# Two small VectorE operations moved to other engines, and three steps moved in the order, in an induced-attention and ELU-FFN kernel

## The chip, the core and the metric

The kernel runs on one core of a Trainium2 chip. Its time is device microseconds (us) of one execution. The core has five engines that each run their own queue in order: TensorE (PE in the profile; its weight loads have a row of their own, PEld), VectorE (DVE), ScalarE (ACT), GpSimd (POOL) and SyncE (SP, which here issues all DMAs). An instruction starts when its engine has come to it and the semaphores that it waits on have arrived; whatever stands behind it in that engine's queue waits too.

## What is computed

```python
# x: 4 x 12480 x 128, inducing: 32 x 128, w_in: 128 x 2048, w_out: 2048 x 128
def mab(q, kv):                                  # attention, 1/sqrt(128) as scale
    s = scale * (q @ kv.T);  s -= s.max(-1)
    a = exp(s);  a /= a.sum(-1) + 1e-9
    return a @ kv
h   = mab(inducing, x)     # first attention:  32 rows look at 12480 tokens -> h: 32 x 128
y   = mab(x, h)            # second attention: every token looks at those 32 rows
g   = elu(y @ w_in)        # 2048 wide
out = g @ w_out            # 49920 x 128, float32
```

x and inducing come as float32, the two weight matrices as float64, which the kernel itself converts to float32 at its start.

## The kernel before, in words

**Tiling.** Each of the four batches is cut into 25 blocks of 512 or 480 tokens, and the blocks are put in 7 groups of 2 to 4 blocks for the attention. The FFN of a block goes in 8 pairs of 128-wide slices of its 2048 columns. A pair is the unit in which the whole program is written: there are 4 x 25 x 8 = 800, numbered n = 0 to 799. The tokens reach the FFN as second-softmax weights (tile `stk`, three stacked parts), and the projected h times w_in is the matrix `hw`, so that `y @ w_in` is one product.

**One pair.** `ffn_in` (L609) is two matmuls into a two-bank PSUM tile `ph`, of which there are three, and an exponential on ScalarE (L617). `ffn_mid` (L623) takes max and min on VectorE. With that the PSUM tile is free again, unless the pair is of kind D. `ffn_split` (L632) makes the high part `gh` on ScalarE. `ffn_low` makes the low part `gl`: on VectorE (L639, kind D) or on GpSimd (L644 and L649, kind P); kind N has no split, and only L644. The kinds of the 8 pairs are `PDNPDPND`. `ffn_out` (L671) is six matmuls (four for N) into the block's PSUM bank `po`, five pairs later; after a block's last pair VectorE transposes the bank (L679) and SyncE sends it out.

**Order.** In iteration n the program issues `ffn_in(n)`, `ffn_mid(n-1)`, `ffn_split(n-1)`, `ffn_low(n-2)`, then goes on with steps that are under way, then `ffn_out(n-5)`, then starts the side steps whose place n/8 has come. A side step is a generator: `yield k` lets it rest for k pairs. The places of side steps are blocks counted from the batch's first, and stand in `attend` and `first_half`. On PE, VectorE and ScalarE the instructions stay in the order in which the program issues them; on GpSimd and SyncE a scheduler at build time may move them.

**Side steps.** For batch b they compute the first attention of batch b+1 and the second attention of groups to come. First attention: `scores` (L310 to L327, running maxima in `pm`), `bias_of` (the maximum over the four copies of a row, brought together by a product `apart` and a matmul with `nsel4`; once after group 2, once after group 6), `weights_of` (exponential, sums in `es`), `e_of` (a transpose), `gather` (L399, 32 small matmuls, then L409, L411 or L416 adds the bank to `h`), `sum_es`, `share_of` (one matmul, then r = 1/(sum + 1e-9) on VectorE, L439 and L440), `norm_h` (L446), `spread_h` (L452, L455), `project_h`, `stack_h`. Second attention, per group: `attend_scores` (L527, L537), `attend_exp`, `attend_norm` (row sum L558, + 1e-9 L559, reciprocal L560, product on GpSimd L561), `attend_stack` (transpose L570, parts L580 and L582, DMAs into `stk`).

**PSUM.** All eight banks are used: three `ph` of two banks, and two `po` banks, which the blocks take in turn. After the opening a side step's matmul goes into the `po` bank that the next block will take (`bank`). So the next block's first `ffn_out` must wait until VectorE has read the side step's result, and a side step must wait until the one before it in the same bank has been read. `po` of block k begins with pair 8k+5.

**Opening.** The first attention of batch 0 and the conversion of the weights are not hidden behind anything. Their steps are written out in the string `FIRST`: x and y are the two transpose halves of a group's tokens, s and m its scores and maxima, w its weights, e its transpose, g and h its gather and the addition; b0 to b2 the biases; A to E the conversion of a piece of a weight matrix (A takes it apart on VectorE and ScalarE, B makes the scale on GpSimd, C puts bits together on VectorE, D multiplies on VectorE and GpSimd, E splits w_out on ScalarE and GpSimd); l0 to l3 the second attention of block 0 alone, a0 to a3 that of the rest of group 0; u0 and on are the pairs, among which the rest of the steps stand. When the string is used up, after some 12 pairs, the list `steady` is filled, and side steps take the other form where a line asks for it.

Of the kernel before, what the change touches and what calls it, by code (L numbers as in the profile page):

```python
# [9 lines left out]
F32 = mybir.dt.float32  # L10
# [3 lines left out]
AF = mybir.ActivationFunctionType  # L14
# [3 lines left out]
P = 128  # L18
# [14 lines left out]


FIRST = """
    A0 A1 B0 x0 y0 C0 B1 x1 s0 D0 y1 C1 m0 s1 D1 x2 m1 y2 x3 s2 m2 y3 b0 w0 s3 x4 w1 m3 e0
    y4 w2 e1 x5 s4 m4 A2 g0 y5 e2 h0 g1 b1 x6 y6 w3 g2 s5 w4 h1 h2 e3 B2 s6 e4 m5 room A3 g3
    m6 b2 B3 g4 h3 w5 w6 C2 e5 D2 sum g5 e6 h4 g6 C3 h5 share h6 D3 norm spread l0 project
    l1 A4 stack l2 A5 l3 B4 a0 u0 a1 C4 B5 u1 a2 D4 C5 u2 E4 a3 D5 A6 u3 B6 E5 u4 C6 u5 D6
    A7 u6 B7 E6 u7 C7 u8 D7 u9 E7 u10 u11 u12  # L40
"""


# [1 line left out]
def kernel(  # L45
# [8 lines left out]
    nc = tc.nc  # L54
# [28 lines left out]
    EPS = 1e-9  # L83
# [9 lines left out]
    const = ctx.enter_context(tc.tile_pool(name="const", bufs=1))  # L93
# [19 lines left out]
    steady = []  # L113

    def bank(name, take=False):
        if not steady and not take:
            return ps_h.tile([P, 2, 512], F32, tag="ph", name=name)[:, 0]
        t = ps_o.tile([P, 512], F32, tag=f"po{turn[0] % 2}", name=name)
        if take:
            turn[0] += 1  # L120
        return t
# [22 lines left out]
    ps = bank("ps_ind")  # L144
# [9 lines left out]
    WS = 512  # L154
    rebias = const.tile([P, 1], F32, name="rebias")
    nc.gpsimd.memset(rebias, -896.0)
    largest = const.tile([P, 1], F32, name="largest")
    nc.gpsimd.memset(largest, 254.0)

# [134 lines left out]
    def start(b):  # L294
        st = dict(
            pm=small.tile([P, NG], F32, tag="pm", name=f"pm_{b}"),
            es=small.tile([P, NG], F32, tag="es", name=f"es_{b}"),
        )
        nc.gpsimd.memset(st["pm"], -3.0e38)
        nc.gpsimd.memset(st["es"], 0.0)  # L300
        state[b] = st
# [31 lines left out]
    def phases(b):  # L333
        ends = [0, 3, NG - 2, NG] if b == 0 else [0, 3, NG]
        return [range(i, j) for i, j in zip(ends, ends[1:])]
# [4 lines left out]
    def bias_of(b, i):  # L340
        st = state[b]
        n = phases(b)[i].stop
        ps = bank(f"ps_pm_{b}_{i}")
        apart = small.tile([P, 4, NG], F32, tag="apart", name=f"apart_{b}_{i}")
        nc.vector.tensor_tensor(
            out=apart[:, :, :n],
            in0=st["pm"][:, :n].unsqueeze(1).broadcast_to([P, 4, n]),
            in1=mine.unsqueeze(2).broadcast_to([P, 4, n]),
            op=ALU.mult,
        )  # L350
        nc.tensor.matmul(ps[:, : 4 * n], nsel4, apart[:, :, :n], start=True, stop=True)
        yield 1
        bias = small.tile([P, 1], F32, tag=f"bias{i}", name=f"bias_{b}_{i}")
        nc.vector.tensor_reduce(out=bias, in_=ps[:, : 4 * n], axis=AX.X, op=ALU.min)
        st["bias", i] = bias
        if i:
            st["scale", i] = small.tile([P, 1], F32, tag=f"scale{i}", name=f"scale_{b}_{i}")
            nc.scalar.activation(
                st["scale", i], st["bias", i - 1], AF.Exp, bias=bias, scale=-1.0
            )  # L360
# [25 lines left out]
    def e_of(b, g):  # L386
        st = state[b]
        np_, T = GROUPS[g][1] * Q, GROUPS[g][2]
        e = ep.tile([P, T], F32, tag="e", name=f"e_{b}_{g}")
        nc.vector.transpose(e[:np_], st["s", g])  # L390
        st["e", g] = e
# [41 lines left out]
    def share_of(b):  # L433
        st = state[b]
        ps = bank(f"ps_es_{b}")
        nc.tensor.matmul(ps[:, :1], sel4, st["es1"], start=True, stop=True)
        yield 1
        r = small.tile([P, 1], F32, tag="r", name=f"r_{b}")
        nc.vector.tensor_scalar_add(r, ps[:, :1], EPS)  # L439
        nc.vector.reciprocal(r, r)  # L440
        st["r"] = r

    def norm_h(b):
        st = state[b]
        hn = once.tile([P, C], F32, tag="hn", name=f"hn_{b}")
        nc.vector.tensor_scalar_mul(hn, st["h"], st["r"])  # L446
        st["hn"] = hn
# [105 lines left out]
    def attend_norm(b, g):  # L553
        s = state[b]["s2", g]
        np_, U = s.shape[:2]
        eng = nc.gpsimd if steady else nc.vector
        sm = small.tile([P, U], F32, tag="sm2", name=f"sm2_{b}_{g}")[:np_]
        nc.vector.tensor_reduce(out=sm, in_=s, axis=AX.X, op=ALU.add)  # L558
        nc.vector.tensor_scalar_add(sm, sm, EPS)  # L559
        nc.vector.reciprocal(sm, sm)  # L560
        eng.tensor_tensor(  # L561
            out=s, in0=s, in1=sm.unsqueeze(2).broadcast_to([np_, U, Q]), op=ALU.mult
        )
        yield 3
# [133 lines left out]
    def first_half(b):  # L698
        steps = [(0.0, lambda: start(b))]
        at = 0.0  # L700
        for g in range(NG):
            for h in [h for h in range(NH) if HALVES[h][2] == g]:

                room = attend(b - 1, HALVES[h - 1][2])[0][0] - (b - 1) * NBLK + 0.3 if h else 0.0
                at = max(at + 0.5, room)
                steps.append((at, lambda h=h: load_xT(b, h)))
            steps.append((at + 1.1, lambda g=g: scores(b, g)))
            if g + 1 == phases(b)[0].stop:
                first = at + 1.1
        second = at + 1.1  # L710
        end = NBLK - 3.97
        for i, (at, till) in enumerate([(first, second), (second, end)]):
            steps.append((at + 0.2, lambda i=i: bias_of(b, i)))
            at += 0.4
            gap = (till - at) / len(phases(b)[i])
            for g in phases(b)[i]:
                steps.append((at, lambda g=g: weights_of(b, g)))
                steps.append((at + 0.15, lambda g=g: e_of(b, g)))
                steps.append((at + 1.19, lambda g=g: gather(b, g)))
                for j, v in enumerate(range(0, GROUPS[g][2] // Q, UP)):  # L720
                    steps.append((at - 0.7 + 0.1 * j, lambda g=g, v=v: load_xm(b, g, v)))
                at += gap
        steps.append((end + 0.3, lambda: room_for_h(b), f"h{b}"))
        steps.append((end + 0.3, lambda: sum_es(b), f"h{b}"))
        steps.append((end + 0.4, lambda: share_of(b), f"h{b}"))
        steps.append((end + 0.6, lambda: norm_h(b), f"h{b}"))
        steps.append((end + 0.8, lambda: spread_h(b), f"h{b}"))
        steps.append((end + 1.1, lambda: project_h(b), f"h{b}"))
        steps.append((end + 1.4, lambda: stack_h(b), f"h{b}"))
        return [((b - 1) * NBLK + v[0], *v[1:]) for v in steps]  # L730
# [150 lines left out]
```

## Time and profile before

| | |
|---|---|
| time, median of 3 runs | 1749.53 us (1749.2 to 1749.7) |
| the profiled execution's own time | 1750.1 us |
| its span, first to last instruction | 1748.3 us |
| mean granted TensorE clock | 0.985 |
| start of pair 0 | 61.2 us |
| time of one batch in the middle (from one stall to the same one in the next batch) | 420.1 us |

A row of a timeline gives start, duration, engine, line, operation, output and inputs, the shapes, the count of merged instructions, and in brackets the time for which the engine had been idle and what it waited for. A row of a group view gives count, busy time and mean duration in ns of one, then the idle time ahead of the group and what ended it. A row of the waits gives total time, times, and the longest one. In the chain of waits "issue" is time in which nothing that the profile shows was waited for. Line numbers are those of the kernel before; in the changed kernel lines are two to nine higher.

### The profile page before, as it was taken

How to read it: one execution, taken by the hardware profiler on the slowest of the kernel's cores; microseconds unless marked ns; L12 is line 12 of the kernel's file. 1: busy time of each engine (PE TensorE's matmuls, PEld its weight loads, DVE VectorE, ACT ScalarE, POOL GpSimd, SP SyncE). 2: the span in 40 equal slices, each digit the busy share in tenths (PEclk: the TensorE clock that was granted, in tenths of full speed). 3: DMA queues.
4: the chain of work that ended last, by engine and by line, in shares of the span. 5: the costliest groups of instructions: out<-in, count | busy, mean ns of one | idle time of the engine just before them, and what ended most of it. 6: DMA issues, size and time to landing. Idle time of an engine off the chain costs nothing.

```text
span 1748.3 us, 22270 instructions
## 1 busy us (share of the span) xinstructions
PE 1652.5 (95%) x7448; PEld 1175.6 (67%) x7448; DVE 1569.1 (90%) x1608; ACT 1384.8 (79%) x1593; POOL 1341.5 (77%) x941
## 2 busy tenths in 40 slices
PE   6589999999999999999999999999999999999998
PEld 4256766767675676667776666666767767676776
DVE  6789999989899999998989999989888999999996
ACT  4468888878787888878787888878878878888886
POOL 4567777877787777877778777877778878887886
PEclk9689999999999999999999999999999999999999
DMA  7254233322225243232323432320312111111111
GB/s 243 47 84 70 59 61 55 61 52 65 66 47 79 36 79 66 41 61 61 79 49 53 62 60 49 77 54 13 79 42 44 36 19 35 28 36 18 35 22 22
DMA packets 384754, 98.10 MB, mean 56 GB/s; under 512 B 364864, under 2 KB 370784, under 8 KB 384384
## 3 DMA queue, kind: packets, MB, share of 16 engines
q1 hardware_dynamic: 384640, 96.68, 28.2%
q8 instruction: 59, 0.97, 0.2%
q14 instruction: 55, 0.45, 0.1%
HBM read 48.94 MB, written 25.56 MB: 43 GB/s over the span
## 4 chain that ended last, share of the span: by engine, by line
PE 74%; DVE 17%; ACT 5%; issue 2%; DMA 1%; POOL 1%; SPq 0%; DVEq 0%; ACTq 0%; POOLq 0%
PE po L671 51%; PE ph L609 18%; DVE e L623 4%; DVE ph L623 3%; ACT e L617 3%; DVE sm L559 2%; DVE gl L639 2%; PE ps_t L527 1%; PE ps_hh L399 1%; ACT gh L632 1%; PE ps_s L310 1%; DVE xT L257 1%; DVE sm L558 1%; PE ps_x L278 1%; DVE pm L327 1%
## 5 line engine op out<-in xcount | busy, mean ns | idle before, releaser
L617 ACT ACTIVATE e<-ph 128x1024 f32<-128x1024 f32 (+1 forms) x800 | 805.0, 1007 | 258.2 <-PE ph L609 249.5
L644 POOL TENSOR_SCALAR e<-e 128x1024 f32<-128x1024 f32 (+1 forms) x500 | 511.0, 1029 | 331.4 <-ACT gh L632 323.5
L649 POOL TENSOR_TENSOR gl<-e,gh 128x1024 fp32r<-128x1024 f32 (+1 forms) x300 | 703.3, 2344 | 16.3
L623 DVE SCALAR_TENSOR_TENSOR e<-ph,e 128x1024 f32<-128x1024 f32 (+1 forms) x500 | 593.3, 1187 | 77.7 <-ACT e L617 76.0
L609 PE MATMUL ph<-stk,hw 128*128 128x512 f32 (+1 forms) x1600 | 561.7, 433 | 45.1 <-DVE e L623 38.2
L671 PE MATMUL po<-gh,wo_h 128*128 128x512 f32 (+1 forms) x1200 | 466.8, 389 | 19.3 <-ACT wo_h L236 9.1
L671 PE MATMUL po<-gh,wo_l 128*128 128x512 f32 (+1 forms) x1200 | 465.8, 388 | 4.2 <-POOL wo_l L237 4.2
L609 PEld LDWEIGHTS ph<-stk,hw 128*128 128x128 f32 x1600 | 291.9, 190 | 226.7 <-DVE e L623 88.6
L623 DVE SCALAR_TENSOR_TENSOR ph<-ph,e 128x1024 f32<-128x1024 f32 (+1 forms) x300 | 358.9, 1196 | 62.7 <-ACT e L617 62.6
L671 PE MATMUL po<-gl,wo_h 128*128 128x512 f32 (+1 forms) x1200 | 368.1, 388 | 0.0
L671 PE MATMUL po<-e,wo_n 128*128 128x512 f32 (+1 forms) x800 | 368.0, 582 | 0.0
L639 DVE SCALAR_TENSOR_TENSOR gl<-ph,gh 128x1024 fp32r<-128x1024 f32 (+1 forms) x300 | 356.0, 1187 | 1.0 <-ACT gh L632 1.0
L632 ACT ACTIVATE gh<-e 128x1024 fp32r<-128x1024 f32 (+1 forms) x300 | 312.1, 1040 | 24.4 <-DVE e L623 24.4
L632 ACT ACTIVATE gh<-ph 128x1024 fp32r<-128x1024 f32 (+1 forms) x300 | 301.1, 1004 | 31.9 <-DVE ph L623 31.6
L671 PEld LDWEIGHTS po<-gh,wo_h 128*128 128x128 f32 x1200 | 226.5, 189 | 67.9 <-ACT wo_h L236 9.5
L671 PEld LDWEIGHTS po<-gh,wo_l 128*128 128x128 f32 x1200 | 226.7, 189 | 49.1 <-POOL wo_l L237 4.9
L671 PEld LDWEIGHTS po<-gl,wo_h 128*128 128x128 f32 x1200 | 226.6, 189 | 43.4 <-POOL gl L649 0.7
L671 PEld LDWEIGHTS po<-e,wo_n 128*128 128x128 f32 x800 | 151.5, 189 | 106.7 <-issue 92.0
L679 DVE STREAM_TRANSPOSE o<-po 128x512 f32<-128x512 f32 (+1 forms) x100 | 68.9, 689 | 4.0 <-PE po L671 4.0
L559 DVE TENSOR_SCALAR sm<-sm 128x16 f32<-128x16 f32 (+3 forms) x28 | 44.9, 1605 | 1.0
L257 DVE STREAM_TRANSPOSE xT<-xq 128x1024 f32<-128x1024 f32 (+2 forms) x39 | 45.4, 1165 | 0.0
L399 PE MATMUL ps_hh<-xm,e 128*32 128x128 f32 (+2 forms) x872 | 32.3, 285 | 2.7 <-DVE e L390 1.6
(96 smaller groups left out, 572.4 us busy)
## 6 DMA issues: line engine op xcount, KB each, us to landing
xm<-in_x_dram SPq DMA_DIRECT2D x32, 512.0 KB, 4.6
out_dram<-o SPq DMA_DIRECT2D x240, 64.0 KB, 2.0
xq<-in_x_dram SPq DMA_DIRECT2D x84, 128.0 KB, 3.7
out_dram<-o SPq DMA_DIRECT2D x160, 60.0 KB, 2.0
stk<-ahi SPq DMA_DIRECT2D x118, 64.0 KB, 2.0
xq<-in_x_dram SPq DMA_DIRECT2D x60, 120.0 KB, 3.4
stk<-ahi SPq DMA_DIRECT2D x80, 60.0 KB, 2.0
stk<-alo SPq DMA_DIRECT2D x59, 64.0 KB, 2.0
```

The source lines that it names most:

```text
L257: nc.vector.transpose(t, xq.rearrange("p u d -> p (u d)"))
L399: nc.tensor.matmul(ps[c * Q : (c + 1) * Q, :C], st["e", g][:np_, u * Q : (u + 1) * Q], st["xm", g, u - u % UP][:np_, u % UP, :], start=(u ...
L559: nc.vector.tensor_scalar_add(sm, sm, EPS)
L609: nc.tensor.matmul(ph[:, i], state[b]["hw"][:, f * P : (f + 1) * P], stacks[b, k], start=True, stop=True,)
L617: nc.scalar.activation(e, ph, AF.Exp, bias=-1.0)
L623: nc.vector.scalar_tensor_tensor(out=v["g"], in0=v["ph"], scalar=1.0, in1=v["e"], op0=ALU.max, op1=ALU.min)
L632: nc.scalar.activation(v["gh"], v["g"], AF.Copy, bias=-1.0)
L639: nc.vector.scalar_tensor_tensor(out=v["gl"], in0=v["g"], scalar=-1.0, in1=v["gh"].bitcast(F32), op0=ALU.add, op1=ALU.subtract,)
L644: nc.gpsimd.tensor_scalar(out=v["e"], in0=v["e"], scalar1=-1.0, scalar2=1.0, op0=ALU.add, op1=ALU.mult)
L649: nc.gpsimd.tensor_sub(v["gl"], v["e"], v["gh"].bitcast(F32))
L671: nc.tensor.matmul(po[:, :T], w, g, start=(cp == 0 and i == 0), stop=(cp == NCP - 1 and i == len(parts) - 1),)
L679: nc.vector.transpose(o.rearrange("p u d -> p (u d)"), po[:, :T])
```

## The change

1. `attend_norm`, after the opening: the addition of 1e-9 is an activation (Identity with a tile `eps` as bias) on ScalarE, one pair after the row sum, and the reciprocal comes one pair after that. In the opening it stays on VectorE. It holds for 27 of 29 calls.
2. `bias_of`, after the opening: the product `apart` runs on GpSimd, and the matmul with what follows it comes three pairs later. It holds for 6 of 9 calls.
3. `first_half`: the first `weights_of` of a phase stands 1.0 block after the phase's start rather than 0.4. The groups of a phase are spread evenly over the rest of it, so all of `weights_of`, `e_of`, `gather` and `load_xm` move by some pairs. `share_of` goes from 0.4 to 0.62 and `norm_h` from 0.6 to 0.75 blocks after the end mark; `spread_h` stays at 0.8.
4. `FIRST` is another order of the same steps.

```diff
@@ FIRST
-    A0 A1 B0 x0 y0 C0 B1 x1 s0 D0 y1 C1 m0 s1 D1 x2 m1 y2 x3 s2 m2 y3 b0 w0 s3 x4 w1 m3 e0
-    y4 w2 e1 x5 s4 m4 A2 g0 y5 e2 h0 g1 b1 x6 y6 w3 g2 s5 w4 h1 h2 e3 B2 s6 e4 m5 room A3 g3
-    m6 b2 B3 g4 h3 w5 w6 C2 e5 D2 sum g5 e6 h4 g6 C3 h5 share h6 D3 norm spread l0 project
-    l1 A4 stack l2 A5 l3 B4 a0 u0 a1 C4 B5 u1 a2 D4 C5 u2 E4 a3 D5 A6 u3 B6 E5 u4 C6 u5 D6
-    A7 u6 B7 E6 u7 C7 u8 D7 u9 E7 u10 u11 u12
+    x0 A0 A1 B0 x1 y0 C0 B1 D0 y1 s0 C1 m0 s1 x2 m1 y2 x3 s2 m2 y3 b0 w0 s3 x4 w1 m3 e0 y4
+    w2 e1 x5 s4 D1 m4 A2 g0 y5 B2 g1 b1 h0 e2 x6 y6 g2 s5 C2 A3 w4 w3 s6 h1 h2 e3 e4 m5 room
+    g3 m6 b2 B3 h3 w5 g4 w6 e5 D2 sum g5 e6 h4 g6 C3 h5 D3 share h6 norm spread l0 A4
+    project l1 A5 l2 l3 B4 B5 a0 stack u0 a1 u1 C4 D4 a2 C5 E4 u2 D5 a3 u3 A6 B6 E5 u4 C6 u5
+    D6 A7 u6 B7 E6 u7 u8 C7 D7 u9 u10 E7 u11 u12
@@ tile_induced_attention__then__elu_ffn_kernel
+    eps = const.tile([P, 1], F32, name="eps")
+    nc.gpsimd.memset(eps, EPS)
@@ bias_of
-        ps = bank(f"ps_pm_{b}_{i}")
         apart = small.tile([P, 4, NG], F32, tag="apart", name=f"apart_{b}_{i}")
-        nc.vector.tensor_tensor(
+        (nc.gpsimd if steady else nc.vector).tensor_tensor(
             out=apart[:, :, :n],
             in0=st["pm"][:, :n].unsqueeze(1).broadcast_to([P, 4, n]),
             in1=mine.unsqueeze(2).broadcast_to([P, 4, n]),
             op=ALU.mult,
         )
+        if steady:
+            yield 3
+        ps = bank(f"ps_pm_{b}_{i}")
         nc.tensor.matmul(ps[:, : 4 * n], nsel4, apart[:, :, :n], start=True, stop=True)
@@ attend_norm
         nc.vector.tensor_reduce(out=sm, in_=s, axis=AX.X, op=ALU.add)
-        nc.vector.tensor_scalar_add(sm, sm, EPS)
+        if steady:
+            yield 1
+            nc.scalar.activation(sm, sm, AF.Identity, bias=eps[:np_])
+            yield 1
+        else:
+            nc.vector.tensor_scalar_add(sm, sm, EPS)
         nc.vector.reciprocal(sm, sm)
@@ first_half
             steps.append((at + 0.2, lambda i=i: bias_of(b, i)))
-            at += 0.4
+            at += 1.0
...
-        steps.append((end + 0.4, lambda: share_of(b), f"h{b}"))
-        steps.append((end + 0.6, lambda: norm_h(b), f"h{b}"))
+        steps.append((end + 0.62, lambda: share_of(b), f"h{b}"))
+        steps.append((end + 0.75, lambda: norm_h(b), f"h{b}"))
         steps.append((end + 0.8, lambda: spread_h(b), f"h{b}"))
```

What this does to the engines' queues is shown at three places.

VectorE's queue at the softmax of batch 0's group 5, in pairs 129 to 133 (`sm2` is the row sum, `e_` and `ph_` with a number are `ffn_mid` of that pair). Before:

```order
L623 SCALAR_TENSOR_TENSOR ph_129_3097<-ph_129_3097,e_129_3100 128x2x480
L558 TENSOR_REDUCE sm2_0_5_3132<-s2_0_5_2871 128x15
L559 TENSOR_SCALAR sm2_0_5_3132<-sm2_0_5_3132 128x15
L560 RECIPROCAL sm2_0_5_3132<-sm2_0_5_3132 128x15
L623 SCALAR_TENSOR_TENSOR e_130_3118<-ph_130_3115,e_130_3118 128x960
L639 SCALAR_TENSOR_TENSOR gl_129_3146<-ph_129_3097,gh_129_3121 128x960
L623 SCALAR_TENSOR_TENSOR e_131_3143<-ph_131_3140,e_131_3143 128x960
```

Now, on VectorE and, in the second piece, on ScalarE:

```order
L632 SCALAR_TENSOR_TENSOR ph_129_3097<-ph_129_3097,e_129_3100 128x2x480
L562 TENSOR_REDUCE sm2_0_5_3130<-s2_0_5_2873 128x15
L632 SCALAR_TENSOR_TENSOR e_130_3116<-ph_130_3113,e_130_3116 128x960
L648 SCALAR_TENSOR_TENSOR gl_129_3141<-ph_129_3097,gh_129_3119 128x960
L632 SCALAR_TENSOR_TENSOR e_131_3138<-ph_131_3135,e_131_3138 128x960
L569 RECIPROCAL sm2_0_5_3130<-sm2_0_5_3130 128x15
```

```order
L626 ACTIVATE e_130_3116<-ph_130_3113 128x960
L641 ACTIVATE gh_129_3119<-ph_129_3097 128x960
L626 ACTIVATE e_131_3138<-ph_131_3135 128x960
L565 ACTIVATE sm2_0_5_3130<-sm2_0_5_3130,eps_131 128x15
L322 COPY s_1_6_3144<-ps_s_1_6_3132 64x480
```

The addition has left VectorE's queue, the reciprocal stands three long instructions behind the sum, and ScalarE has the addition behind `gh` of pair 129 and the exponential of pair 131.

PE's queue at pairs 84 and 85, where block 9 ends and block 10 begins (`po_0_10` is block 10's first product). Before:

```order
L609 MATMUL ph_84_2285<-stk4_141,hw_0_510 128x512 x2
L671 MATMUL po_0_9_2155<-gh_79_2195,wo_h_127 128x512
L671 MATMUL po_0_9_2155<-gh_79_2195,wo_l_128 128x512
L671 MATMUL po_0_9_2155<-gh_79_2195,wo_h_127 128x512
L671 MATMUL po_0_9_2155<-gh_79_2195,wo_l_128 128x512
L671 MATMUL po_0_9_2155<-gl_79_2229,wo_h_127 128x512 x2
L609 MATMUL ph_85_2302<-stk4_141,hw_0_510 128x512 x2
L671 MATMUL po_0_10_2319<-gh_80_2227,wo_h_127 128x512
```

Now:

```order
L618 MATMUL ph_84_2269<-stk4_143,hw_0_517 128x512 x2
L680 MATMUL po_0_9_2157<-gh_79_2197,wo_h_127 128x512
L680 MATMUL po_0_9_2157<-gh_79_2197,wo_l_128 128x512
L680 MATMUL po_0_9_2157<-gh_79_2197,wo_h_127 128x512
L680 MATMUL po_0_9_2157<-gh_79_2197,wo_l_128 128x512
L680 MATMUL po_0_9_2157<-gl_79_2214,wo_h_127 128x512 x2
L403 MATMUL ps_hh_1_1_2286<-xm_1_1_0_2021,e_1_1_2121 32x128 x8
L403 MATMUL ps_hh_1_1_2286<-xm_1_1_8_2023,e_1_1_2121 32x128 x8
L618 MATMUL ph_85_2303<-stk4_143,hw_0_517 128x512 x2
L680 MATMUL po_0_10_2321<-gh_80_2212,wo_h_127 128x512
```

The gather of group 1, which stood at pair 80, now stands at pair 84, one pair ahead of the block that takes its bank next. The gather of group 3 went from pair 143 to pair 148 in the same way (block 18 begins at 149), and both recur in each of three batches.

PE's queue at `share_of` (`ps_es`) for batch 1. Before:

```order
L671 MATMUL po_0_20_3797<-gl_167_3854,wo_h_127 128x480 x2
L436 MATMUL ps_es_1_3940<-es1_1_3922,sel4_110 128x1
L609 MATMUL ph_173_3942<-stk3_139,hw_0_510 128x480 x2
L671 MATMUL po_0_21_3962<-gh_168_3852,wo_h_127 128x480
L671 MATMUL po_0_21_3962<-gh_168_3852,wo_l_128 128x480
```

Now:

```order
L680 MATMUL po_0_21_3959<-gl_169_3899,wo_h_127 128x480 x2
L440 MATMUL ps_es_1_3982<-es1_1_3923,sel4_110 128x1
L618 MATMUL ph_175_3984<-stk3_141,hw_0_517 128x480 x2
L680 MATMUL po_0_21_3959<-e_170_3871,wo_n_126 128x480 x2
L456 MATMUL ps_ht_1_4000<-sel4_110,hn_1_3998 128x128
```

The share has gone from the pair ahead of block 21's first product to two pairs into that block, and `spread_h` (`ps_ht`), which stays, now follows it after one pair. In the same way `bias_of`'s matmul goes from pairs 40 and 132 to pairs 43 and 135; pair 132 is the one ahead of block 16's first product.

## The prediction

> **What bounds the kernel now.** I read the page first, then the waits of PE, then windows, then the timeline around single waits.
>
> ```profile
> PE 1652.5 (95%) x7448; PEld 1175.6 (67%) x7448; DVE 1569.1 (90%) x1608; ACT 1384.8 (79%) x1593; POOL 1341.5 (77%) x941
> PE po L671 51%; PE ph L609 18%; DVE e L623 4%; DVE ph L623 3%; ACT e L617 3%; DVE sm L559 2%; DVE gl L639 2%; PE ps_t L527 1%; PE ps_hh L399 1%; ACT gh L632 1%; PE ps_s L310 1%; DVE xT L257 1%; DVE sm L558 1%; PE ps_x L278 1%; DVE pm L327 1%
> ```
>
> PE sets the pace, and VectorE has the rest of the chain that ended last, the second line. One entry there is strange: L559 adds a constant to a 128x16 tile, and 2% of the span hangs on it. The windows separate the opening (pair 0 starts at 61.2 us; from 110 us on the pattern repeats):
>
> ```profile
> 0.00:61.20 61.20, 39.19 (x404) 25.32 (x404) 39.42 (x85) 22.47 (x46) 28.32 (x37) 0.86 0.57 185
> 110.00:1748.30 1638.30, 1582.86 (x6965) 1131.74 (x6964) 1488.02 (x1481) 1332.77 (x1501) 1279.58 (x874) 1.00 0.27 51
> ```
>
> The columns are length, then busy time of PE, PEld, DVE, ACT, POOL, and the granted clock. From 110 us on PE is idle for 1638.3 - 1582.9 = 55.4 us, at clock 1.00. The waits of PE in that window are all on VectorE:
>
> ```profile
> PE ph L609 <- DVE e L623: 33.1, 27, 1.7
> PE ps_pm L351 <- DVE apart L345: 6.6, 6, 1.2
> PE po L671 <- DVE r L439: 5.4, 3, 1.8
> PE po L671 <- DVE s L537: 2.6, 4, 0.7
> PE po L671 <- DVE bias L354: 2.2, 3, 0.7
> ```
>
> They sum to 49.9 us. The change touches four of the five rows, so it can gain at most some 47 us there, and a little for slow starts behind each wait.
>
> **The addition of 1e-9.** Here is one stall, on VectorE, GpSimd and PE:
>
> ```profile
> 293.15 0.64 DVE L558 TENSOR_REDUCE sm<-s 128x15 f32<-128x480 f32 x1
> 293.83 2.27 DVE L559 TENSOR_SCALAR sm<-sm 128x15 f32<-128x15 f32 x1
> 293.71 2.36 POOL L649 TENSOR_TENSOR gl<-e,gh 128x1024 fp32r<-128x1024 f32 x1
> 293.90 1.88 PE L671 MATMUL po<-e,wo_n 128*128 128x512 f32 x4
> 297.51 0.73 PE L609 MATMUL ph<-stk,hw 128*128 128x512 f32 x2 [1.74 <-DVE e L623]
> 298.08 0.39 PE L671 MATMUL po<-gh,wo_h 128*128 128x512 f32 x1
> 597.86 0.17 DVE L559 TENSOR_SCALAR sm<-sm 128x16 f32<-128x16 f32 x1
> 598.07 0.25 DVE L560 RECIPROCAL sm<-sm 128x16 f32<-128x16 f32 x1
> 598.07 2.38 POOL L649 TENSOR_TENSOR gl<-e,gh 128x1024 fp32r<-128x1024 f32 x1
> L559 DVE TENSOR_SCALAR sm<-sm 128x16 f32<-128x16 f32 (+3 forms) x27 | 44.8, 1658 | 0.9
> ```
>
> L559 starts just after a GpSimd product `gl` and ends with it: 2.27 us. Where the product starts later (598.07) it takes 0.17. So it is no work but a wait for GpSimd. Alone, 27 would cost 27 x 0.17 = 4.6 of the 44.8 us; 40 us are waiting. What PE loses is less, since three `ph` tiles give slack. Twenty of the 27 waits in the first row of the list follow an L559, the first and last being
>
> ```profile
> 133.17 0.73 PE L609 MATMUL ph<-stk,hw 128*128 128x512 f32 x2 [1.35 <-DVE e L623]
> 1670.69 0.70 PE L609 MATMUL ph<-stk,hw 128*128 128x480 f32 x2 [1.65 <-DVE e L623]
> 301.44 0.45 PE ph L609 x2
> 303.77 1.72 PE po L671 x4
> ```
>
> and they make 28.0 of its 33.1 us. Idle time understates it. The last two rows, of the chain, show undisturbed PE: at 293.90 the four N products would pass in 1.72 us, so `ph` would come at 295.62; it comes at 297.51 and takes 0.57 to the next start rather than 0.45. That is 2.0 us lost for 1.74 idle, 0.27 more. 28.0 + 20 x 0.27 = **33.4 us**, between bounds of 28.0 and the 40 us of waiting. The sum L558 and the reciprocal remain: the one at 598.07 runs beside a product in 0.25, so it will not take over the wait.
>
> On ScalarE 27 short activations come in; the nearest row, a 128x1 activation with a tile as bias, took 294 ns, together 8 us of an engine busy for 79%. It stands behind `gh` of pair 129, which needs `ffn_mid` of 129, and the row sum is the next instruction after that on VectorE (0.64 us against 1.0 for `gh`), so it does not wait for VectorE. The reciprocal stands behind `ffn_mid` of 131, which runs 1.2 us while the addition takes 0.3. I cost both at nothing; if that cover fails, it is the slower rival below. The product L561 and the transpose come two pairs later, still inside the 7.4 pairs that most groups have between steps.
>
> **The product `apart`.** Six PE waits, 6.6 us, plus 6 x 0.27: **8.2 us**. On GpSimd a 128x12 or 128x28 product isn't in the trace; it lies between nothing and the 128x128 product L237 (640 ns), say 0.3, since it has a tenth to a fifth of the elements. Six times that is nothing beside GpSimd's idle 23%, and PE meets it three pairs, some 5.5 us, later, while one product ahead in the queue is 2.4 us.
>
> ```profile
> L358 ACT ACTIVATE scale<-bias,bias 128x1 f32<-128x1 f32 x5 | 1.5, 294 | 2.8 <-DVE bias L354 2.8
> L237 POOL TENSOR_TENSOR wo_l<-w_raw,wo_h 128x128 fp32r<-128x128 f32 x12 | 7.4, 640 | 2.9 <-ACT wo_h L236 2.8
> 451.53 0.45 PE L671 MATMUL po<-gh,wo_h 128*128 128x480 f32 x1 [1.80 <-DVE r L439]
> 453.75 0.49 DVE L446 TENSOR_SCALAR hn<-h,r 128x128 f32<-128x128 f32 x1
> ```
>
> **Bias and share at other places.** Each stood one pair ahead of a block's first product in the same bank; now the bias of pair 132 has six pairs, the share of 172 has six. Gains 2.2 + 3 x 0.27 = **3.0** and 5.4 + 3 x 0.27 = **6.2 us**. The share now comes one pair ahead of `ps_ht`, and r, its reciprocal and hn must run between `ffn_mid` and that matmul: 0.11 + 0.16 + 0.49. `ffn_mid` of the pair ends some 1.1 us after PE's next start, PE reaches `ps_ht` after 0.4 + 1.6 us, so 0 to 0.3 short; I take **1 us** for three. In the row above hn ran beside a product and took 0.49, in the opening 0.28. The Trainium skill (SBUF — State Buffer, Who interferes with whom) says that a VectorE tensor_scalar in a two-port mode and a GpSimd instruction exclude each other for the whole instruction; by it hn could stand behind a whole 2.4 us product, three times, and the sum would come out 6 us higher. The traced hn lost 0.2 at most, and I keep the 1.
>
> **The gathers** go by the same rule the other way: those of groups 1 and 3 now stand one pair ahead of a block's first product, in three batches, six in all. What stands there before:
>
> ```profile
> 265.61 1.23 DVE L623 SCALAR_TENSOR_TENSOR ph<-ph,e 128x1024 f32<-128x1024 f32 x1 [0.99 <-ACT e L617]
> 266.75 0.71 DVE L679 STREAM_TRANSPOSE o<-po 128x512 f32<-128x512 f32 x1
> 265.68 0.63 PE L609 MATMUL ph<-stk,hw 128*128 128x512 f32 x2
> 318.56 1.08 PE L399 MATMUL ps_hh<-xm,e 128*32 128x128 f32 x32
> L416 DVE TENSOR_TENSOR h<-h,ps_hh 128x128 f32<-128x128 f32 x19 | 5.1, 271 | 0.6 <-PE ps_hh L399 0.6
> ```
>
> With 1.0 us of gather put ahead of PE's 265.68, block 10's first product would be due at some 267.2; VectorE's addition ends at 266.75 + 0.71 + 0.28 = 267.75. So 0.5 idle and 0.27, six times: **4.5 us** lost. Bounds: nothing, and 1.8 + 0.27 each as for r, 12 us.
>
> **The opening.** These steps of the chain of waits are moved:
>
> ```profile
> 38.83 0.61 DVE w_part L196
> 39.47 0.72 DVE w_raw L200
> 46.99 0.61 DVE w_raw L206
> 57.74 0.57 issue
> 58.31 0.88 DVE w_part L172
> PE po L671 <- ACT wo_h L236: 9.1, 1, 9.1
> ```
>
> A5 (57.74 to 59.19, 1.45) now comes before l2, where VectorE waits for an exponential anyway; D3 (0.61) falls in a wait for the share; C2 (1.33) goes ahead of e3, which has part of it hidden (0.6); D1 (0.68) moves the other way, into a stretch where VectorE is on the chain; and with x0 in front, A0 and A1 wait for its copies, and with them B0, B1, C0, C1, which I put at 0.5 ahead of b0. Sum -1.45 - 0.6 - 0.6 + 0.1 + 0.5 = -2.0. In the ramp D4's product now stands ahead of the first `gl` on GpSimd, so PE's 9.1 us for `wo_h` shrink by up to 2.4, of which the later weight pieces, unchanged in their amount, take most back. I say **-2.5** in all, from -6 to +3.
>
> **Sum.** 1750.1 - 33.4 - 8.2 - 3.0 - 6.2 - 2.5 + 4.5 + 1 = 1702.3. The profiled execution is 0.6 above the median of its runs, so 1702.
>
> **Rivals.** *GpSimd or another engine becomes the bound.* With the stalls gone PE's five pairs between `ffn_in` and `ffn_out` get shorter, and `gl` may be late. Now:
>
> ```profile
> L671 PEld LDWEIGHTS po<-gl,wo_h 128*128 128x128 f32 x1200 | 226.6, 189 | 43.4 <-POOL gl L649 0.7
> ```
>
> PE's weight loads waited for `gl` for 0.7 us in 1200, all told, so there is room; but VectorE, at 90%, may stay the bound in the stretches where its transposes of `xT`, `pm` and `s` cluster. If half of the 33.4 stays: 1719.
>
> *The new places cost more than they free.* Gathers at 2.1 each (12.4) and hn at 2.4 (7): 1702 + 8 + 6 = 1716. For it: these waits were each 0.7 to 1.8 before. Against: a gather itself holds PE for 1 us, in which VectorE catches up.
>
> *The change does not do what it says:* the wait falls on the next instruction, the reciprocal. Then 1702 + 33 = 1735. Four reciprocals that ran beside a product in 0.25 speak against it.
>
> *Slower:* ScalarE, in order, meets the addition before VectorE has done its sum, and the exponentials behind it wait; VectorE already waits 76 us for ScalarE's exponential in one form of `ffn_mid` alone, so a delay there passes on at once.
>
> ```profile
> DVE e L623 <- ACT e L617: 76.0, 168, 1.1
> ```
>
> It decides from (1750 - 1702) / 27 = 1.8 us of wait each; at 2.4, a whole product's time, 1702 + 65 = 1767. Against it: the order shown, where `gh` covers the sum.
>
> **How the numbers follow.** Forecast 0.72; VectorE or GpSimd still the bound 0.13; places cost more 0.07; wait moves on 0.04; slower 0.04. The forecast's own range is 1692 (33.4 at 37, opening -6, gathers free) to 1713 (28 for the addition, opening +3, gathers at 1.0 each). The range of 8 in 10 takes in the first two rivals: 1692 to 1719. A measurement here tells 0.2%, 3.5 us, from no change. Faster is all but the last case and a part for what I have overlooked: 0.93, same 0.02, slower 0.05.
>
> **What would show it.** Right: the waits of PE from 110 us on sum to 10 to 15 us, with no row for `apart`, r or bias, a new row of about 3 us for `po` on `h`, and none for `ps_ht`; L565 at 0.3 us on ScalarE and the reciprocal at 0.25. Wrong: reciprocals near 2 us; a row of `po` on `gl`; ScalarE idle ahead of L565; the start of pair 0 after 61.2.

## The result, and the profile after

The changed kernel takes 1711.83 us (1710.70 to 1712.99 in four runs) against 1749.62 us, a ratio of 0.9783 with a 95% interval of 0.9766 to 0.9800. It gains 37.8 us where 47.8 were predicted: inside the range, and 10 us off the forecast. The stalls went as forecast. Something else came in that the prediction didn't have.

The page of the changed kernel, its first line of busy time and the lines of the chain:

```profile
PE 1656.3 (97%) x7448; PEld 1176.5 (69%) x7448; DVE 1522.5 (89%) x1575; ACT 1390.6 (81%) x1620; POOL 1342.3 (78%) x948
PE po L680 62%; PE ph L618 20%; ACT e L626 2%; DVE e L632 1%; PE ps_s L312 1%; PE ps_t L531 1%; PE ps_hh L403 1%; DVE ph L632 1%; ACT gh L641 1%; DMA xm<-in_x_dram 1%; DVE o L688 1%; DVE w_part L198 1%; DVE gl L648 0%; DMA w_raw<-in_moe_w_in_dram 0%; PE ps_hw L467 0%
```

The addition and the row sum, 2% and 1% of the chain before, are not among these lines any more. The waits of PE from 110 us on, of the changed kernel:

```profile
PE ph L618 <- DVE e L632: 4.2, 8, 0.9
PE po L680 <- DVE s L541: 2.3, 4, 0.7
PE po L680 <- DVE h L415: 0.8, 3, 0.3
PE po L680 <- DVE h L420: 0.8, 3, 0.3
```

They sum to 8.1 us, where the same view of the kernel before had 49.9 and the prediction 10 to 15. The rows of `apart`, the bias and r are gone, and the two rows of the gathers (`h`) are new, 1.6 us together. The addition, now on ScalarE, and the reciprocal, by their tile, with minimum, median and maximum in ns:

```profile
L565 ACT ACTIVATE sm<-sm,eps x27: 294/297/329, 126.2 to 1632.5; 128x16 f32<-128x16 f32 x11, 128x15 f32<-128x15 f32 x8, 96x16 f32<-96x16 f32 x4, 64x15 f32<-64x15 f32 x4
L569 DVE RECIPROCAL sm<-sm x28: 218/240/248, 72.6 to 1634.3; 128x16 f32<-128x16 f32 x11, 128x15 f32<-128x15 f32 x8, 96x16 f32<-96x16 f32 x5, 64x15 f32<-64x15 f32 x4
```

So far everything is as forecast. The windows are where it isn't. From 110 us to the end of the changed kernel:

```profile
110.00:1710.80 1600.80, 1587.45 (x6974) 1134.37 (x6966) 1440.82 (x1449) 1338.72 (x1529) 1281.81 (x880) 1.00 0.27 52
```

PE is idle for 1600.8 - 1587.5 = 13.3 us, 42 less than the 55.4 before. But it is *busy* for 4.6 us more than in the window before (1582.9), at the same clock of 1.00 and with the same number of matmuls but for nine. So matmuls have become slower, and the groups by shape show which. First the kernel before, then the changed kernel, both from 110 to 1697 us (the number after the comma is the mean of one in ns):

```profile
L671 PE MATMUL po<-gh,wo_l 128*128 128x512 f32 x708 | 277.1, 391 | 0.0
L671 PE MATMUL po<-gl,wo_h 128*128 128x512 f32 x708 | 219.1, 391 | 0.0
```

```profile
L680 PE MATMUL po<-gh,wo_l 128*128 128x512 f32 x708 | 280.2, 396 | 0.0
L680 PE MATMUL po<-gl,wo_h 128*128 128x512 f32 x708 | 221.7, 394 | 0.0
```

These durations overlap; what counts is the distance from one start to the next. In the trace its median for the 512-column matmuls of `gh` and `gl` goes from 227 to 233 ns (680 pairs of starts with `gh` between 150 and 1680 us). Single distances spread over some 224 to 236 ns, but three quarters of them are 228 ns or less in the kernel before and none in the changed one. For the 480-column matmuls the median goes from 216 to 219; the four N products, in plain float32, stay at 428 and 429. The two medians of `gh` are the same in every quarter of that stretch. Nothing in the diff touches these matmuls.

### The profile page after: what moved, and what is told of

It is laid out like the page before. It is cut to its first block, busy times and chain, and to the rows that moved or that the text cites. A ratio compares the mean times of both kernels' runs of the same rounds, so it can differ in the third digit from the quotient of the medians.

```text
span 1710.8 us, 22335 instructions
## 1 busy us (share of the span) xinstructions
PE 1656.3 (97%) x7448; PEld 1176.5 (69%) x7448; DVE 1522.5 (89%) x1575; ACT 1390.6 (81%) x1620; POOL 1342.3 (78%) x948
## 4 chain that ended last, share of the span: by engine, by line
PE 87%; DVE 7%; ACT 3%; issue 2%; DMA 1%; POOL 0%; SPq 0%; DVEq 0%; ACTq 0%
PE po L680 62%; PE ph L618 20%; ACT e L626 2%; DVE e L632 1%; PE ps_s L312 1%; PE ps_t L531 1%; PE ps_hh L403 1%; DVE ph L632 1%; ACT gh L641 1%; DMA xm<-in_x_dram 1%; DVE o L688 1%; DVE w_part L198 1%; DVE gl L648 0%; DMA w_raw<-in_moe_w_in_dram 0%; PE ps_hw L467 0%
## 5 line engine op out<-in xcount | busy, mean ns | idle before, releaser
L618 PEld LDWEIGHTS ph<-stk,hw 128*128 128x128 f32 x1600 | 295.4, 189 | 188.9 <-issue 84.9
L570 POOL TENSOR_TENSOR s<-s,sm 128x512 f32<-128x512 f32 (+3 forms) x27 | 27.7, 1027 | 19.3 <-DVE sm L569 19.3
L403 PEld LDWEIGHTS ps_hh<-xm,e 128*32 128x32 f32 (+2 forms) x872 | 24.6, 115 | 16.9 <-issue 12.3
```

What stands on the lines that cost most here:

```text
L403: nc.tensor.matmul(ps[c * Q : (c + 1) * Q, :C], st["e", g][:np_, u * Q : (u + 1) * Q], st["xm", g, u - u % UP][:np_, u % UP, :], start=(u ...
L570: eng.tensor_tensor(out=s, in0=s, in1=sm.unsqueeze(2).broadcast_to([np_, U, Q]), op=ALU.mult)
L618: nc.tensor.matmul(ph[:, i], state[b]["hw"][:, f * P : (f + 1) * P], stacks[b, k], start=True, stop=True,)
```

## The experiments

Two questions were open: what slows PE's matmuls, and what each part of the change is worth. Every kernel here does the whole computation. The kernel before ran 15 to 21 times beside each group of kernels, from 1746.6 to 1751.6 us; a difference of 2 us between medians therefore says little. The ratios are formed against the runs beside each kernel and can differ from the quotient of two medians by 0.1%. A second measure is the time from the start of pair 16 to the start of pair 790, which leaves out the opening. It is from one trace each: four kernels whose instructions between these pairs are the same, or differ in the form of one addition alone (before, new opening, unused tile ahead of the weights, addition as a tensor_tensor), lie between 1600.9 and 1603.5 us, so less than some 3 us isn't resolved by it either.

| kernel | median us | ratio to before (95%) | pair 16 to 790, us |
|---|---|---|---|
| before | 1749.6 | 1 | 1602.0 |
| changed | 1711.83 | 0.9783 (0.9766 to 0.9800) | 1563.2 |
| changed, one more unused constant | 1705.75 | 0.9761 (0.9747 to 0.9774) | 1558.5 |
| changed, both constants in one tile | 1700.18 | 0.9723 (0.9710 to 0.9736) | 1553.2 |
| changed, old opening | 1710.26 | 0.9784 (0.9770 to 0.9797) | 1563.4 |
| before, one unused constant | 1760.76 | 1.0072 (1.0059 to 1.0084) | 1614.7 |
| before, unused tile ahead of `gh` | 1758.36 | 1.0060 (1.0044 to 1.0076) | 1610.5 |
| before, unused tile ahead of the weights | 1748.81 | 0.9994 (0.9985 to 1.0003) | 1603.5 |
| before, new opening | 1750.06 | 1.0005 (0.9996 to 1.0014) | 1600.9 |
| before, addition on ScalarE | 1709.95 | 0.9775 (0.9762 to 0.9789) | 1562.5 |
| before, share and gathers moved | 1751.84 | 1.0013 (1.0004 to 1.0022) | 1604.2 |
| before, `apart` on GpSimd, gathers moved | 1746.81 | 0.9985 (0.9976 to 0.9994) | 1599.4 |
| before, addition as a tensor_tensor | 1747.58 | 0.9994 (0.9985 to 1.0003) | 1602.0 |
| one tile, old opening, gathers earlier | 1698.22 | 0.9713 (0.9699 to 0.9726) | 1551.2 |

### Is it the new tile's place in memory?

The one thing the change adds that every later tile feels is `eps`: a constant of 4 bytes that takes 32 in the layout of SBUF (the memory that holds all tiles but those in PSUM) and moves all tiles allocated behind it, `gh`, `gl`, `stk` and `hw` among them, but not the weights `wo_h` and `wo_l`, which are ahead of it. The first edit adds a second such tile to the changed kernel, the second one to the kernel before:

```diff
+    pad = const.tile([P, 1], F32, name="pad")
+    nc.gpsimd.memset(pad, 0.0)
     largest = const.tile([P, 1], F32, name="largest")
```

> The changed kernel with one more small constant tile, used by nobody, beside the new one. All later tiles lie 32 bytes further. Theory A, the place of the tiles in SBUF: the new constant tile moved gh, gl and all behind it by 32 bytes, and so made PE's fp32r matmuls of 512 columns 233 ns apart instead of 227; with the second tile they stand again as far from a multiple of 64 bytes as before, the interval is 227, and some 6000 such matmuls at 4 to 6 ns less give 1698 to 1702 us. Theory B, PE is slower because it runs with fewer breaks: the interval stays at 233 and the time at 1712.

> The kernel before with one more small constant tile, used by nobody, in the place where the change has its own. Theory A (place of the tiles): PE's intervals go from 227 to 233 ns with all stalls left as they were, 1755 to 1763 us, less what the stalls absorb. Theory B (fewer breaks): 227 ns and 1750.

The kernel before got slower by 11 us from a tile that nobody uses. Its groups by shape:

```profile
L673 PE MATMUL po<-gh,wo_l 128*128 128x512 f32 x708 | 280.3, 396 | 0.0
L673 PE MATMUL po<-gl,wo_h 128*128 128x512 f32 x708 | 221.7, 394 | 0.0
```

396 and 394, as in the changed kernel, with all the stalls still there. Theory B, that PE slows because it has fewer breaks, is out. The changed kernel with a second tile came down to 1705.75 only, half of the way, where Theory A had 1698 to 1702: a quarter of its intervals are 228 ns or less, most of the others 231 to 234. So a shift of 64 bytes isn't the same as none. The next edit shifts nothing at all: `eps` becomes the second column of the tile of `rebias`.

```diff
-    rebias = const.tile([P, 1], F32, name="rebias")
+    two = const.tile([P, 2], F32, name="rebias")
+    rebias, eps = two[:, 0:1], two[:, 1:2]
     nc.gpsimd.memset(rebias, -896.0)
-    eps = const.tile([P, 1], F32, name="eps")
     nc.gpsimd.memset(eps, EPS)
```

> The changed kernel with the new constant in the second column of the tile of the older constant, so that every other tile has the very address that it has in the kernel before. Theory A (addresses decide PE's interval): the fp32r matmuls of 512 columns stand 227 ns apart as in the kernel before, 1698 to 1703 us. Theory C, the new order of the instructions has a part in it: between 228 and 233 ns and 1703 to 1708 us, as the changed kernel with one more constant tile (1705.8).

1700.18 us, 11.65 less than the changed kernel, with the same instructions in each queue. Its groups by shape and its window:

```profile
L680 PE MATMUL po<-gh,wo_l 128*128 128x512 f32 x708 | 277.0, 391 | 0.0
L680 PE MATMUL po<-gl,wo_h 128*128 128x512 f32 x708 | 219.0, 390 | 0.0
```

```profile
110.00:1698.00 1588.00, 1572.39 (x6963) 1132.86 (x6961) 1440.50 (x1446) 1333.99 (x1528) 1279.46 (x879) 1.00 0.28 52
```

Theory A holds and C falls: with the old addresses the new order of instructions runs at 227 ns. PE's busy time is now 10.5 us *below* the kernel before, which fits fewer slow starts behind fewer stalls. Over the same work, pair 16 to pair 790, PE is busy for 1555.6 us with `eps` in a tile of its own and for 1542.8 with the shared one, and idle for 7.7 and 10.4: the tile makes the matmuls 12.8 us slower, and 2.7 of that comes out of idle time. Of the 11.65 us, 10.0 lie in this stretch; the rest lies mostly ahead of it, where single traces differ by as much.

### Which address?

Two more shifts of 32 bytes in the kernel before: one of `gh`, `gl` and the output buffers alone, one of everything from the weights on.

```diff
+    padp = ctx.enter_context(tc.tile_pool(name="padp", bufs=1))
     ghp = ctx.enter_context(tc.tile_pool(name="ghp", bufs=GHB))
...
+    pad = padp.tile([P, 1], F32, name="pad")
+    nc.gpsimd.memset(pad, 0.0)
```

```diff
+    pad = const.tile([P, 1], F32, name="pad")
+    nc.gpsimd.memset(pad, 0.0)
     win_sb = const.tile([C, F], F32, name="win_sb")
```

> The kernel before with an unused 4-byte tile just ahead of the buffers of gh: gh, gl and the output buffers lie 32 bytes further, everything else (weights, stk, hw, xT, e) where it was. If it is the addresses of PE's moving operand gh and gl: 233 ns as with the unused constant, about 1760. If it is one of the other tiles that the unused constant moved (stk, hw, xT, e, and what the other engines read and write): 227 ns and 1750.

> The kernel before with an unused 4-byte tile ahead of the weights: the weights wo_h, wo_l, win_sb and all behind them lie 32 bytes further, so that the distance of the weights from gh and gl is as before and every address from the weights on is 32 bytes off. If the distance between weights and moving operand counts: 227 ns and 1750. If the own address of gh and gl counts: 233 ns and about 1760.

Moving `gh` and `gl` alone costs 8 us; moving the weights along with them costs nothing. Here are `gh` and `gl` 32 bytes off, then all 32 bytes off:

```profile
L674 PE MATMUL po<-gh,wo_l 128*128 128x512 f32 x708 | 278.9, 394 | 0.0
L674 PE MATMUL po<-gl,wo_h 128*128 128x512 f32 x708 | 222.9, 395 | 0.0
```

```profile
L673 PE MATMUL po<-gh,wo_l 128*128 128x512 f32 x706 | 276.0, 391 | 0.0
L673 PE MATMUL po<-gl,wo_h 128*128 128x512 f32 x707 | 218.7, 390 | 0.0
```

The last kernel has `gh` and `gl` at the very place where they were slow and runs at 227 ns. So it is not the place of the moving operand itself, but its distance from the weights: they are the only operands of these matmuls whose distance from `gh` and `gl` changes in both slow kernels and in neither of the fast ones. Of the distances tried, the one of the kernel before is good, 32 bytes more is bad, 64 bytes more is half bad; no other was tried. Moving everything behind the weights cost 11.1 us, `gh` and `gl` alone 8.0, but the intervals of the two ratios overlap, so it isn't shown that the other tiles cost anything.

The Trainium skill (SBUF — State Buffer, Who interferes with whom) gives TensorE two read ports of its own, one for the moving operand and one for the weight load, calls them independent, and says that TensorE never waits on anyone. By that a shift would cost nothing. The 8 to 11 us measured here for a change of distance speak against it for these operands; by what mechanism, no run shows.

### The parts one by one

**The addition on ScalarE alone**, with the shared tile, so that no address moves:

```diff
-        nc.vector.tensor_scalar_add(sm, sm, EPS)
+        if steady:
+            yield 1
+            nc.scalar.activation(sm, sm, AF.Identity, bias=eps[:np_])
+            yield 1
+        else:
+            nc.vector.tensor_scalar_add(sm, sm, EPS)
```

> The kernel before with the addition of 1e-9 on ScalarE and nothing else; the constant shares a tile, so that no address moves. The prediction has 33.4 us for this part: 1716 at 1750. Counted from the two traces, some 1.85 us at each of 20 waits: 1713. The rival that another engine becomes the bound in these stretches: 1733. If the new places of the changed kernel are needed for it: above 1720.

It alone gains 39.6 us, more than any of these forecasts had, and as much as the whole change (37.8; the intervals of the two ratios overlap). Its waits of PE from 110 us on and its window:

```profile
PE po L678 <- DVE r L441: 5.4, 3, 1.8
PE ps_pm L353 <- DVE apart L347: 4.7, 6, 1.2
PE ph L616 <- DVE e L630: 4.0, 5, 1.0
PE po L678 <- DVE s L539: 2.6, 4, 0.7
PE po L678 <- DVE bias L356: 2.2, 3, 0.7
```

```profile
110.00:1707.90 1597.90, 1574.31 (x6964) 1134.58 (x6963) 1444.70 (x1452) 1335.12 (x1528) 1278.62 (x873) 1.00 0.28 52
```

The row of `ph` fell from 33.1 us in 27 waits to 4.0 in 5. Idle time fell by 55.4 - 23.6 = 31.8 us, busy time by 1582.9 - 1574.3 = 8.6. With 22 fewer waits, each wait had cost 0.39 us beyond its idle time, if all of the 8.6 is put down to them.

**Share, norm and gathers at their new places**, and nothing else:

```diff
-            at += 0.4
+            at += 1.0
...
-        steps.append((end + 0.4, lambda: share_of(b), f"h{b}"))
-        steps.append((end + 0.6, lambda: norm_h(b), f"h{b}"))
+        steps.append((end + 0.62, lambda: share_of(b), f"h{b}"))
+        steps.append((end + 0.75, lambda: norm_h(b), f"h{b}"))
```

> The kernel before with the bias, the share and the normalizing of h at their new places and nothing else. By the prediction -3.0 -6.2 +4.5 +1 = -3.7, 1746. With what the trace of the changed kernel shows for the gathers (1.6 us idle and 6 x 0.27 for the restarts) -3.0 -6.2 +3.2 = -6.0, 1744.

It was slower by 2 us (interval 0.7 to 3.9), where both estimates had it faster. One error is the estimates' own: the bias isn't moved by this edit, but by the three pairs that `bias_of` waits for GpSimd. The rest is in the waits from 110 us on:

```profile
PE ph L609 <- DVE e L623: 34.6, 31, 1.7
...
PE po L671 <- DVE bias L354: 2.2, 3, 0.7
PE ps_ht L452 <- DVE hn L446: 1.7, 3, 0.6
PE po L671 <- DVE h L411: 0.9, 3, 0.3
PE po L671 <- DVE h L416: 0.8, 3, 0.3
```

r's 5.4 us are gone. In their place stand 3.4 us of idle in nine new waits (hn and the gathers), and 1.5 us in four more waits on e. At 0.39 of restart for each, 13 waits more and 3 fewer come to 3.9: -5.4 + 3.4 + 1.5 + 3.9 = +3.4. Between pair 16 and pair 790 it is 2.2, the same within what one trace resolves.

**The product `apart` on GpSimd, three pairs ahead**, with the gathers moved, which the later bias needs:

> The kernel before with the bias's product on GpSimd, its matmul three pairs later, and the exponentials of the second half begun 0.6 of a block later, which the later bias needs; the sum L559 and the share stay as before. The prediction has -8.2 for the product and -3.0 for the bias; the gathers, which move too, give back 3.2 by the trace of the changed kernel (4.5 by the prediction): -8.0 and 1741.5 (1743 by the prediction). If freeing these waits only hands their time to the next wait on e: 1747 or more.

-3.6 us by the medians (-1.0 to -4.2 by the ratio) rather than -8. Its waits from 110 us on, the start of block 21's first product behind the share (450 us), the additions, still on VectorE, and one of them with the product beside it:

```profile
PE ph L611 <- DVE e L625: 39.2, 34, 1.7
PE po L673 <- ACT e L619: 3.2, 3, 1.1
...
450.04 0.45 PE L673 MATMUL po<-gh,wo_h 128*128 128x480 f32 x1 [1.08 <-ACT e L619]
...
L561 DVE TENSOR_SCALAR sm<-sm 128x16 f32<-128x16 f32 (+3 forms) x28 | 51.8, 1849 | 1.0
...
175.62 2.23 DVE L561 TENSOR_SCALAR sm<-sm 128x16 f32<-128x16 f32 x1
175.47 2.35 POOL L651 TENSOR_TENSOR gl<-e,gh 128x1024 fp32r<-128x1024 f32 x1
```

The rows of `apart` and the bias are gone, 8.8 us, and the wait at the share is 1.08 us each rather than 1.80, put down to another releaser. But the additions now take 51.8 us where the kernel before had 44.9 for the same 28. Three of them, at 176.90 us and at the same place in the next two batches, took 0.17 us before, with the product starting just behind them; now it starts just ahead of them, and they take 2.23. PE waits 6.1 us longer, in seven more waits, for the e that comes later. With the two rows of the gathers (1.7, not shown), -8.8 - 2.2 + 6.1 + 1.7 = -3.2 us of idle are left. So part of what one edit frees is lost to a wait that another edit removes: this part and the places alone make -3.6 and +2.3, with the moved gathers in both; behind the addition on ScalarE, all the rest together (1709.95 to 1700.18) makes -9.8.

**The opening**, the new `FIRST` in the kernel before, and the old one in the changed kernel:

> The kernel before with the new order of the opening and nothing else. From the two traces: pair 0 starts at 66 us instead of 61.2, and the ramp makes up all but 1.1 us of it by pair 14, so 1750.5 to 1751.5. The prediction's working would have it at 1747.

> The changed kernel with the old order of the opening. If the opening's delay passes on unchanged, 1 us less than the changed kernel (1710.5 to 1711); if the ramp is set by the weights and not by the start, no difference; by the prediction's working 2.5 us more.

No difference that can be measured in the first, 1.6 us less in the second, with ranges of 1710.2 to 1710.8 and 1710.7 to 1713.0. Pair 0 starts at 61.2 us before, 66.3 in the changed kernel, 63.9 with the shared tile and 63.2 with the new order alone; pair 16 at 115.8, 116.9, 114.4 and 114.4. All kernels with the new order start pair 0 later than those with the old one, and some 15 pairs later almost nothing is left of it.

### Why does the addition wait?

The prediction read from overlap alone that the addition waits for GpSimd. If the cause is the form of the instruction, another form on VectorE would not wait:

```diff
-        nc.vector.tensor_scalar_add(sm, sm, EPS)
+        nc.vector.tensor_tensor(
+            out=sm, in0=sm, in1=eps[:np_].broadcast_to([np_, U]), op=ALU.add
+        )
```

> The kernel before with the addition still on VectorE, as a product of two tensors' form (tensor_tensor, adding the constant from a tile) in place of the form with a number (tensor_scalar); no address moves. Theory D, it is the form that shuts VectorE out while GpSimd runs a product: the addition takes 0.2 us at once, no wait, and 20 stalls vanish, 1713 to 1718. Theory E, whatever small instruction stands there waits for GpSimd: 1.7 us on average as before, 1749.

The same time as before. The timeline around one of them, at the place that the prediction showed:

```profile
293.03 0.65 DVE L560 TENSOR_REDUCE sm<-s 128x15 f32<-128x480 f32 x1
293.58 2.36 POOL L653 TENSOR_TENSOR gl<-e,gh 128x1024 fp32r<-128x1024 f32 x1
293.71 2.27 DVE L561 TENSOR_TENSOR sm<-sm,rebias 128x15 f32<-128x15 f32 x1
296.01 0.25 DVE L564 RECIPROCAL sm<-sm 128x15 f32<-128x15 f32 x1
```

A sum with a tile waits for the product as long as one with a number, 2.27 us both, and all 28 take 44.9 us in either form. Theory D falls. Theory E says too much, though: the reduction and the reciprocal on the same engine don't wait (0.65 beside the start of a product, 0.25 beside the four products that a reciprocal met in the kernel before). The Trainium skill (SBUF — State Buffer, Who interferes with whom) has a rule that fits all of them: a VectorE instruction with two inputs in SBUF contends with a GpSimd instruction that reads SBUF, one with a single input contends only in a two-port mode, and tensor_reduce never. The trace agrees: 2.27 us for the two-input form and for tensor_scalar, 0.65 and 0.25 for the others; that this tensor_scalar runs in a two-port mode is argued from its wait, no run shows the mode. The same section says that ScalarE never waits on anyone, and the trace agrees here too: the addition on ScalarE took 294 to 329 ns in all 27 places.

### A kernel that beats both

The shared tile with the old opening, and the gathers put where none stands one pair ahead of a block's first product:

```diff
-            at += 1.0
+            at += 0.7
```

> The changed kernel with the constants in one tile (addresses of the kernel before), the old order of the opening, and 0.7 instead of 1.0 of a block between the bias and the gathers, which puts no gather one pair ahead of a block's first product. From 1700.2 for the shared tile: -1.5 for the opening (1711.8 against 1710.3 where it alone was undone) and -3.3 for the six gathers (1.7 us of waits and 6 x 0.27): 1695.4. If the gathers cost as much at the earlier places: 1698.5.

1698.22 us. The waits of PE from 110 us on:

```profile
PE ph L618 <- DVE e L632: 4.0, 5, 1.0
PE po L680 <- DVE s L541: 2.6, 4, 0.7
PE ps_ht L456 <- DVE hn L450: 1.7, 3, 0.6
```

The gathers' rows are gone as expected; between pair 16 and pair 790 it is 2.0 us faster than the shared tile alone, where 3.3 were expected, and one trace each doesn't resolve that. The opening gave nothing: pair 16 starts 1.5 us later than with the new order. Against the shared tile alone the intervals of the two ratios overlap, so the two are not told apart; both are 10 us or more faster than the changed kernel.

## Why the prediction was right, and where it was off

The direction and the mechanism were right, and the time fell inside the range. That it did is in part luck: the 10 us by which it missed the forecast come from something that no term or rival of the prediction stood for. Compared at equal addresses (1700.18 against a forecast of 1702), the sum came out within 2 us, but that is luck too: one term was too small by 6 us, the others together too large by 5. The forecast's own range, 1692 to 1713, is also a little narrower than its parts, which add up to 1690 to 1714.

- **The addition, 33.4: undersized.** Alone it gains 39.6. The idle part was nearly right (28.0 of the waits on e were put down to it, 29.1 went, and 1.9 of those on `apart`). One of the twenty waits was misread: the one at 133.17 comes almost 9 us after the last L559 has ended, and half of it was left when the addition had moved; the first that follows an L559 is the one of 0.52 at 125.74, which makes 27.2. The start after a wait was taken as 0.27 us from one example at 293.90; over 22 waits it is 0.39.
- **`apart` 8.2, bias 3.0, share 6.2: the waits were right, all three rows are gone from the changed kernel.** The product on GpSimd took 222 ns, where 0.3 us was estimated. But with the gathers, hn and the opening these terms were to make -8.2 - 3.0 - 6.2 + 4.5 + 1 - 2.5 = -14.4 behind the addition, and made -9.8.
- **The gathers, 4.5: right in kind.** Six waits, 0.27 us each, where 0.5 was estimated; with a restart of 0.39 each that would be about 4.
- **hn, 1: wrong in how, and 1 in neither layout.** In the changed kernel hn ran at 288 ns, and PE shows no row for `ps_ht`. With the shared tile it took 1.1 us three times, and PE waited 1.7. Rows of the timelines of both, shared tile first, then of the kernel before:

```profile
1255.38 1.95 POOL L653 TENSOR_SCALAR e<-e 128x960 f32<-128x960 f32 x2
1256.30 1.11 DVE L450 TENSOR_SCALAR hn<-h,r 128x128 f32<-128x128 f32 x1
```

```profile
1264.63 2.03 POOL L653 TENSOR_SCALAR e<-e 128x960 f32<-128x960 f32 x2
1265.52 0.29 DVE L450 TENSOR_SCALAR hn<-h,r 128x128 f32<-128x128 f32 x1
```

```profile
451.89 2.27 POOL L649 TENSOR_TENSOR gl<-e,gh 128x960 fp32r<-128x960 f32 x1
453.75 0.49 DVE L446 TENSOR_SCALAR hn<-h,r 128x128 f32<-128x128 f32 x1
```

  In the new kernels hn meets two GpSimd instructions of about 1 us each. In the first case it ends with the second of them (1257.41 and 1257.33), in the second it ends soon after the change from one to the other. The row by which the prediction set the rule aside is no evidence against it: of that product only 0.4 us were left when hn started, and hn ended with it (454.24 and 454.16). So the rule that the prediction weighed fits all three; what it costs depends on which GpSimd instruction is there and how much of it is left, and that is one of 1 us, not the product of 2.4.
- **The opening, -2.5: not found.** Pair 0 started at 66.3 us, and a start after 61.2 was named as a sign that the prediction is wrong. It was one for this term; the time came back in the ramp, and the new order alone changed nothing that can be measured.
- **The rivals.** No engine became the bound: GpSimd is at 78%, and the waits of PE are 8.1 us. The reciprocal did not take over the wait (218 to 248 ns). None of PE's waits from 110 us on is for ScalarE. Of the rival that the new places cost more than they free, the runs bear out a part: alone they cost 2 us, and what they do behind the addition was not measured apart from `apart` and the bias.
- **The step that failed** is one that the prediction did not have: it costed the new constant's tile at nothing without saying so. Of the edits it named every instruction that moved, but not what an allocation moves. That tile costs 11.65 us between the medians, 10.0 between pair 16 and pair 790, measured by putting its constant into another tile. A tally from the groups by shape gives the size of the 12.8 us by which PE is busy longer: 708 x (5 + 4 + 4) ns = 9.2 us for the 512-column products of `gh` and `gl`, and some 3 us for the 480-column ones. Why 32 bytes of distance slow these matmuls stays open.

## What to carry to other kernels

When PE is the bound, compare its mean duration per shape before and after, even for matmuls that the change doesn't touch: an edit that adds a tile can move operands. Put a new small constant into a tile that is already there, and if matmul times change without cause, shift the moving operand against the weights by 32 bytes at a time. Measure an edit's parts on top of the largest one: while the additions still stood on VectorE, a small edit made three more of them meet a product, and lost there part of what it freed.

## What had not been expected of the hardware

- A tile of 4 bytes that nobody uses made this kernel 0.7% slower. Matmuls on fp32r operands with 512 columns start 227 ns or 233 ns apart in the median, depending on the distance in SBUF between weights and moving operand; those on plain float32 operands show no such difference (428 and 429 ns).
- In no layout is the interval one value: of these intervals three quarters are 228 ns or less in the kernel before, none with 32 bytes of shift, a quarter with 64. What decides it for a single matmul is open.
- A VectorE addition of 128x16 with two inputs stands behind a GpSimd product for up to 2.27 us, as one with an immediate does, while a reduction (0.65) or a reciprocal (0.25) passes.
